# Finishing rows 0 to 3 of a batch during row 7's first pass, and rows 4 to 7 together at the end, in a cached-attention decode kernel

## The chip, the cores and the metric

The kernel runs on one core of a Trainium2 chip. The time is the device time of the program in microseconds (us), as a median of several executions. A profiled execution also has a span, from its first to its last instruction, which is about 2 us shorter than the device time of the same execution. In the lines of the profile PE is TensorE, which does the matmuls, PEld its weight loads, DVE is VectorE, ACT ScalarE, POOL GpSimd, and SP issues the loads.

## The reference

Two identical layers are applied to x, which has 8 batch rows of one token with 448 features. Each layer is an attention over a cache and then a mixer with two small MLPs.

```python
def A(x, k_cache, v_cache, wq, wo):      # caches: 8 rows x 8 kv heads x 4096 x 256, bf16
    q = (x @ wq).reshape(8, 1, 16, 256)  # 16 query heads, 2 per kv head
    p = softmax(q k^T / 16)              # per row and head, over 4096 positions
    return (p v).reshape(8, 1, 4096) @ wo

def B(x, w1, w2, w3, w4):
    ...                                  # hs is zero here: each shift of a 1-token sequence pads it away
    x1 = x + hs
    return x1 + gelu(layernorm(x1) @ w3) @ w4

for _ in range(2):
    x = x + A(layernorm(x), k_cache, v_cache, wq, wo)
    x = x + B(layernorm(x), w1, w2, w3, w4)
return x
```

Both layers read the same caches. The query of the second layer depends on the whole first layer of the same row, so each row's cache is passed over twice. Rows are independent of each other.

## The kernel before

The caches are cut into chunks of 1 MB (128 partitions of 4096 bf16 values). For a pair of kv heads there are 4 key chunks and 4 value chunks. All chunks go through 15 slots in SBUF. A list of items, one per chunk, alternates a key chunk of one pair with a value chunk of the pair before. A slot goes to the next load when its chunk has been used. For each row, 12 of the 32 chunks of the first pass stay in slots (or in PSUM) until the second pass, and so are loaded only once.

```python
kept = [(GP - 1, kv, n) for n in range(4) for kv in range(2)] + [(GP - 2, 0, n) for n in range(3)]
...
for b in range(Bn):                      # (pass, row, pair of kv heads)
    tasks += [(1, b, gp) for gp in keep[::-1]]
    if b + 1 < Bn:
        tasks += [(0, b + 1, gp) for gp in keep]
    if b == Bn - 2:
        tasks += [(1, Bn - 3, free[-1])]
    ...
```

Work that is not tied to a chunk is written as Python generators and is dealt out in pieces between the items. `chain` takes a row from the first pass to the query of the second. `last` ends the attention of a row's second pass. `rest` finishes rows: the product with wo, the normalization, w3, tanh (as gelu), w4. In this kernel it does so for rows 0 to 6 together, begins when row 6 has finished its second pass, and so runs among the chunks of row 7's second pass.

```python
def rest(b, st):
    nb = Bn - 1
    yield from out_cols(lambda i: OT2[:, i % 2, i // 2, :nb], wo_sb, NB2, 0, nb, 1)   # 160 matmuls
    yield from mlp(0, nb)                                                          # 56 with w3, 70 with w4
    ...                                    # 4 matmuls turn the result into rows
    nc.sync.dma_start(out[:nb].rearrange("b s d -> (b s) d"), xo)
...
elif done == 4 and not final:
    add_gen("last", b, last(b, st), idx + 1, idx + (7 if b == Bn - 2 else 13), 6)
    if b == Bn - 2:
        add_gen("last", 0, rest(b, st), idx + 1, len(items) - 2, 21)
```

A row's normalization takes its reciprocal root on POOL, as a power:

```python
nc.vector.tensor_scalar(ve[:, 0], var, 0.0, EPS, ALU.max, ALU.add)
if twice:
    nc.vector.tensor_scalar(ve[:, 1], var, 0.0, EPS * EPS / (1 + EPS), ALU.max, ALU.add)
nc.gpsimd.tensor_tensor(rs[:, 0:n] ..., ve[:, 0:n] ..., nhalf[:].to_broadcast([128, n * nb]), ALU.pow)
```

After the last chunk, row 7 alone goes through what I call the tail: scaling, the last quarter of its wo product, normalization, w3, tanh, w4, and the output.

```python
xs = xT[:, :, Bn - 1 : Bn]
nc.vector.tensor_add(xs, xs, st["y"])
ident2 = ...; nc.vector.tensor_copy(ident2, identb[:])
nc.vector.memset(o_row, 0.0)
HT = run(mlp_hidden(Bn - 1, 1))
...                                        # 14 matmuls with xT, 56 with HT and w4, into o_row
nc.vector.tensor_copy(xo, o_row)
nc.sync.dma_start(out[Bn - 1] ..., xo ...)
```

The softmax here doesn't subtract the row's maximum and nothing guards it: scores larger than these inputs give would overflow.

Of the kernel before, what the change touches and what calls it, by code (L numbers as in the profile page):

```python
# [17 lines left out]
def kernel(  # L18
# [56 lines left out]

    spare = [slots[-1], slots[-2]]

    def scratch(a, n):
        return spare[0][:].bitcast(FP32)[:, a : a + n]

# [26 lines left out]
        ALU.add,  # L107
    )

    ptw = consts.tile([128, 4, 16, 14], BF16, name="ptw")  # L110
    nc.vector.memset(ptw[:], 0.0)

    misc = psum.tile([128, 512], FP32, name="misc")
    ot_bank = misc[:, 256:320]
# [6 lines left out]
    def room_ps(what, nb):  # L121

        at, n = {"y": (320, 8), "st": (336, 2), "h": (352, HC), "q": (384, NB2)}[what]
        if nb == 1:
            return misc[:, at : at + n]
        at, n = {"y": (0, 8), "st": (64, 2), "h": (80, HC), "q": (256, NB2)}[what]
        return store[0 if nb == Bn else 1][:, at : at + n * nb]

    wv = consts.tile([128, 4], FP32, name="wv")
    nc.vector.memset(wv[:, 0:3], 1.0 / D)  # L130
# [1 line left out]
    one = consts.tile([128, 1], FP32, name="one")  # L132
    nc.vector.memset(one[:], 1.0)
    ones = one[:].to_broadcast([128, 128])
    nhalf = consts.tile([128, 1], FP32, name="nhalf")
    nc.vector.memset(nhalf[:], -0.5)
    xb = {}
# [53 lines left out]
    def norm(x, nb, twice):  # L191
# [2 lines left out]

        def room(name, shape, at):
            n = shape[0] * shape[1]
            if nb == 1:
                t = chn.tile([128, n], FP32, tag=name)
                ap = t[:]
            else:  # L200
                ap = scratch(at, n * nb)
            return ap.rearrange("p (s f b) -> p s f b", s=shape[0], f=shape[1])
# [140 lines left out]
    def mlp_hidden(b0, nb):  # L343

        yield from norm(xT[:, :, b0 : b0 + nb], nb, True)
        h_ps = room_ps("h", nb)
        for c in range(HC):
            for fc in range(4):
                w, xi = wblk(w3_sb, F, c, fc)
                nc.tensor.matmul(  # L350
                    h_ps[:, c * nb : c * nb + nb],
                    w,
                    xbs(nb)[:, xi, :],
                    start=(fc == 0),
                    stop=(fc == 3),
                )
            if c == HC // 2:
                yield
        yield
        if nb == 1:  # L360
            g_t = chn.tile([128, 2, HC], FP32, tag="g")
            HT_t = chn.tile([128, HC, 1], BF16, tag="HT")
            hh, g0, HT = g_t[:, 0], g_t[:, 1], HT_t[:]
        else:
            hh, g0 = scratch(64, HC * nb), scratch(640, HC * nb)
            HT = scratch(256, HC * nb // 2).bitcast(BF16).rearrange("p (c b) -> p c b", b=nb)

        nc.vector.tensor_scalar_mul(hh, h_ps, 0.5)
        nc.vector.scalar_tensor_tensor(g0, hh, 2 * 0.044715, h_ps, ALU.mult, ALU.mult)
        nc.vector.scalar_tensor_tensor(g0, g0, 1.0, h_ps, ALU.add, ALU.mult)  # L370
        nc.scalar.activation(g0, g0, ACT.Tanh, scale=0.7978845608028654)
        yield
        nc.vector.scalar_tensor_tensor(
            HT.rearrange("p c b -> p (c b)"), g0, 1.0, hh, ALU.add, ALU.mult
        )
        yield
        return HT

# [84 lines left out]
    def first_last(b, st):  # L463

        yield from half(st["o", 1], st["z"], 1, OT2[:, :, :, b])
        if b == Bn - 1:
            yield from add_cols(
                st["y"],
                lambda i: OT2[:, i % 2, i // 2, b : b + 1],
                wo_sb,  # L470
                range(NB2 // 2, NB2),
                2,
                open=(claim(st), False),
            )
# [5 lines left out]
    def last(b, st):  # L480
        yield from half(st["o", 0], st["z"], 0, OT2[:, :, :, b])

    def rest(b, st):

        nb = Bn - 1
        yield from out_cols(lambda i: OT2[:, i % 2, i // 2, :nb], wo_sb, NB2, 0, nb, 1)
        yield from mlp(0, nb)
        xh = scratch(768, 2 * nb).bitcast(BF16).rearrange("p (c b) -> p c b", c=4)
        nc.vector.tensor_copy(xh, xT[:, :, :nb])
        yield  # L490
        o_row = store[0][:nb, 0:D]
        for fc in range(4):
            w = 128 if fc < 3 else 64
            nc.tensor.matmul(
                o_row[:, 128 * fc : 128 * fc + w], xh[:w, fc, :], identb[:w, :w], start=True, stop=True
            )
        yield
        xo = scratch(1024, D // 2).bitcast(BF16)[:nb]
        nc.vector.tensor_copy(xo, o_row)
        nc.sync.dma_start(out[:nb].rearrange("b s d -> (b s) d"), xo)  # L500



    keep = sorted({gp for gp, _, _ in kept})
    free = [gp for gp in range(GP) if gp not in keep]
    assert Bn > 2 and free == [0, 1] and GP == 4
    tasks = [(0, 0, gp) for gp in free + keep] + [(0, 1, gp) for gp in free]


# [115 lines left out]
    def pv(o_ps, v, a, gp, begin):  # L625


        g = 2 * gp + a // 2
        w = 6 - 2 * (g % 4)
        for y in range(16):  # L630
            q = y % 4
            nc.tensor.matmul(  # L632
                o_ps[32 * q : 32 * q + 8, 0:256],
                ptw[:, a, 4 * (y % 4) + y // 4, w : w + 8],
                v[:, y * Dh : (y + 1) * Dh],
                start=(begin and y < 4),
                stop=(y >= 12),
                skip_group_check=True,
            )
# [40 lines left out]

    def step(idx):

        for kind in ("chain", "last"):
            e = next((e for e in gens if e["kind"] == kind), None)
            if e is None:
                continue
            if e["n"] == 0:
                e["at"] = max(e["at"], idx)
            if e["n"] < e["of"] * (idx - e["at"] + 1) / max(e["until"] - e["at"], 1):
                e["n"] += 1  # L690
                if next(e["g"], gens) is gens:
                    gens.remove(e)

    first_of = {}
    for idx, (n, kv, c) in enumerate(items):
        first_of.setdefault((tasks[n][:2], kv), idx)
    yF, rz_gp, at_end = None, None, False

    for idx, it in enumerate(items):
        n, kv, c = it  # L700
        ps, b, gp = tasks[n]
        p = where[(b, gp), (kv, c)] if ps == 1 and (stays(it) or inside(it)) else where[it]
        slot = slots[p]
        final = (ps, b) == (1, Bn - 1)
        if kv == 0:
# [11 lines left out]
            if "z" not in st:  # L717
                z_t = chn.tile([128, 2, GP], FP32, tag="zall", bufs=3)
                st["z"] = z_t
                if final:  # L720
                    st["y"] = store[2][:, 0:4].unsqueeze(2)
                    oc = store[3][:, 0 : 2 * Hq].rearrange("p (j h) -> p j h", j=2)
            if not (ps == 1 and stays(it)):
                transpose_k(slot)
# [12 lines left out]
        else:  # L737
# [6 lines left out]
            if final and gp in free:  # L744
                pv_cols(oc, slot, c, gp)
                if c % 2 == 1:
# [4 lines left out]
                    run(  # L751
                        add_cols(
                            st["y"],
                            lambda i: OT2[:, i % 2, i // 2, b : b + 1],
                            wo_sb,
                            range(h0, h0 + 4),
                            5,
# [14 lines left out]
            if c == 3:  # L772
# [3 lines left out]
                elif done == 2:  # L776
                    add_gen("chain" if final else "last", b, first_last(b, st), idx + 1, idx + 13, 9)
                elif done == 4 and ps == 0:
                    add_gen("chain", b, chain(b, st), idx + 1, first_of[(1, b), 0] - 1, 30)
                elif done == 4 and not final:  # L780
                    add_gen("last", b, last(b, st), idx + 1, idx + (7 if b == Bn - 2 else 13), 6)
                    if b == Bn - 2:
                        add_gen("last", 0, rest(b, st), idx + 1, len(items) - 2, 21)
        if not (ps == 0 and stays(it)):
            if (ps, gp, kv, c) == (1, keep[-1], 0, 0):
                kept_place = p
            elif final and stays(it) and at_end is not None:

                if not at_end:
                    at_end, spare[:] = True, []  # L790
                spare.append(slot)
                if len(spare) == 2:
                    at_end = None
            else:
                places.append(p)
        emit_loads()
# [2 lines left out]
        step(10 * len(items))  # L799


    xs = xT[:, :, Bn - 1 : Bn]
    nc.vector.tensor_add(xs, xs, st["y"])
    ident2 = spare[1][:, 0:256].bitcast(FP32)
    nc.vector.tensor_copy(ident2, identb[:])
    W = D // 4
    o_row = store[0][:, 0:W]
    nc.vector.memset(o_row, 0.0)
    HT = run(mlp_hidden(Bn - 1, 1))
    for q in range(4):  # L810
        for fc in range(4):
            w = 128 if fc < 3 else 64
            lo, hi = max(W * q, 128 * fc), min(W * q + W, 128 * fc + w)
            if lo < hi:
                nc.tensor.matmul(
                    o_row[32 * q : 32 * q + 1, lo - W * q : hi - W * q],
                    xT[:w, fc, Bn - 1 : Bn],
                    ident2[:w, lo - 128 * fc : hi - 128 * fc],
                    start=(lo == W * q),
                    stop=False,  # L820
# [2 lines left out]
    for c in range(HC):  # L823
        for q in range(4):
            nc.tensor.matmul(
                o_row[32 * q : 32 * q + 1, :],
                HT[:, c, :],
                w4_sb[:, c, W * q : W * q + W],
                start=False,
                stop=(c == HC - 1),  # L830
                skip_group_check=True,
            )
    xo = spare[1][:, 256 : 256 + W]
    nc.vector.tensor_copy(xo, o_row)
    nc.sync.dma_start(
        out[Bn - 1].rearrange("s (q w) -> (s q) w", q=4),
        xo.rearrange("(q r) w -> q r w", r=32)[:, 0, :],
    )


# [28 lines left out]
```

## Time and profile before

| | before |
|---|---|
| device time, median of the 3 runs known for the prediction | 1141.98 us (1140.06 to 1143.87) |
| span of the profiled execution | 1133.7 us |
| last value chunk landed | 1113.3 us |
| its matmuls began, ended | 1121.0, 1122.0 us |
| from there to the end (the tail) | 11.7 us |

The first lines are from the page: the span in 40 slices of 28.3 us, with TensorE's and the DMA engines' busy tenths and the rate of the loads, and the shares of the chain of waits that ended last.

```profile
PE   3145677557764666556764576737665576557786
DMA  9999999999999999999999999999999999999992
GB/s 350 369 421 420 413 369 384 418 417 377 404 419 412 395 398 419 420 408 391 410 419 420 407 393 395 420 419 386 412 418 420 406 379 407 419 417 370 412 419 93
...
DMA 63%; PE 15%; DVE 13%; issue 4%; SPq 3%; ACT 1%; POOL 1%; POOLq 0%; DVEq 0%; ACTq 0%
```

Loading bounds the kernel. The DMA engines are busy in every slice but the last. A chunk lands every 2.5 us at 420 GB/s, and the rate dips to between 369 and 395 GB/s about once per row. TensorE is busy about six tenths. So the time can only change through the landing of the last chunk, or through what comes after it.

These are lines of the timeline of the end: start, duration, engine, line of the kernel, operation, operands, count, and in brackets the idle time of the engine before them. L646 is the value product of the last pairs (32 matmuls a chunk), L332 the product with wo.

```profile
1112.67 0.51 PE L646 MATMUL store<-ptw,slot 128*128 128x2 bf16 x14 [1.79 <-issue]
...
1115.76 1.01 PE L646 MATMUL store<-ptw,slot 128*128 128x2 bf16 x32
...
1118.08 1.01 PE L646 MATMUL store<-ptw,slot 128*128 128x2 bf16 x32
...
1120.10 1.87 PE L646 MATMUL store<-ptw,slot 128*128 128x2 bf16 x64
...
1122.22 0.82 PE L332 MATMUL store<-qT,wo_sb 128*128 128x1 bf16 x20 [0.26 <-DVE qT L410]
...
1125.51 0.70 POOL L236 TENSOR_TENSOR t<-t,nhalf 128x2 f32<-128x2 f32 x1 [35.31 <-DVE t L243]
...
1130.83 0.28 DVE L834 CAST slot<-store 128x112 bf16<-128x112 f32 x1 [1.58 <-PE store L825]
```

The four last value chunks landed at 1105.3, 1107.8, 1110.2 and 1113.3 us. The matmuls of the four last value chunks start at 1115.8, 1118.1, 1120.1 and 1121.0 us, with no bracket that names a load. TensorE is 7.7 us late for the last chunk. From 1122.0 us on, a serial chain runs to the end.

What TensorE waited for in the last row, from 1060 us to the end, with total, number and longest wait (the four largest):

```profile
PE sc L577 <- issue: 4.4, 3, 1.8
PE misc L350 <- DVE xb L253: 1.9, 1, 1.9
PE store L646 <- issue: 1.8, 1, 1.8
PE store L332 <- issue: 1.8, 2, 1.3
```

No load is among them, nor among the smaller ones. "issue" is time without any wait that the profile shows; experiment e9 looks at it.

### The profile page before, as it was taken

How to read it: one execution, taken by the hardware profiler on the slowest of the kernel's cores; microseconds unless marked ns; L12 is line 12 of the kernel's file. 1: busy time of each engine (PE TensorE's matmuls, PEld its weight loads, DVE VectorE, ACT ScalarE, POOL GpSimd, SP SyncE). 2: the span in 40 equal slices, each digit the busy share in tenths (PEclk: the TensorE clock that was granted, in tenths of full speed). 3: DMA queues.
4: the chain of work that ended last, by engine and by line, in shares of the span. 5: the costliest groups of instructions: out<-in, count | busy, mean ns of one | idle time of the engine just before them, and what ended most of it. 6: DMA issues, size and time to landing. Idle time of an engine off the chain costs nothing.

```text
span 1133.7 us, 36989 instructions
## 1 busy us (share of the span) xinstructions
PE 704.3 (62%) x17177; PEld 509.5 (45%) x17177; DVE 593.8 (52%) x1007; ACT 124.3 (11%) x362; POOL 15.6 (1%) x25
## 2 busy tenths in 40 slices
PE   3145677557764666556764576737665576557786
PEld 2123455335543445344542454525444355436566
DVE  5145454545555554646465554645555455555462
ACT  0001001110200011000110011101010101010110
POOL 0000000000000000000000000000000000000000
PEclk9999998655755558555565556555575557555655
DMA  9999999999999999999999999999999999999992
GB/s 350 369 421 420 413 369 384 418 417 377 404 419 412 395 398 419 420 408 391 410 419 420 407 393 395 420 419 386 412 418 420 406 379 407 419 417 370 412 419 93
DMA packets 67199, 449.15 MB, mean 396 GB/s; under 512 B 6871, under 2 KB 12902, under 8 KB 13414
## 3 DMA queue, kind: packets, MB, share of 16 engines
q1 hardware_dynamic: 67046, 446.80, 97.6%
q8 instruction: 134, 2.20, 0.8%
q14 instruction: 19, 0.16, 0.0%
HBM read 446.77 MB, written 0.01 MB: 394 GB/s over the span
## 4 chain that ended last, share of the span: by engine, by line
DMA 63%; PE 15%; DVE 13%; issue 4%; SPq 3%; ACT 1%; POOL 1%; POOLq 0%; DVEq 0%; ACTq 0%
DMA slot<-in_A_k_cache_dram 59%; DVE slot L569 11%; PE sc L577 5%; DMA slot<-in_A_v_cache_dram 4%; PE o L632 3%; SPq L152 2%; PE misc L332 2%; PE store L332 1%; DMA wq_sb<-in_A_wq_dram 1%; SPq L561 1%; PE misc L350 1%; PE store L646 1%; DVE qbd L304 1%; ACT p_n L586 0%; PE misc L278 0%
## 5 line engine op out<-in xcount | busy, mean ns | idle before, releaser
L569 DVE STREAM_TRANSPOSE slot<-slot 128x1024 uint32<-128x1024 uint32 x400 | 472.8, 1222 | 337.1 <-DMA slot<-in_A_k_cache_dram 322.6
L577 PE MATMUL sc<-slot,qbd 128*8 128x128 bf16 x8192 | 277.5, 286 | 322.9 <-DVE slot L569 260.3
L577 PEld LDWEIGHTS <-qbd 128*8 128x8 bf16 x8192 | 188.5, 105 | 409.6 <-issue 214.6
L632 PE MATMUL o<-slot,ptw 128*8 128x256 bf16 x3968 | 242.5, 386 | 54.6 <-DMA slot<-in_A_v_cache_dram 27.2
L586 ACT ACTIVATE p_n<-sc 128x256 bf16<-128x256 f32 x128 | 95.6, 747 | 736.7 <-PE sc L577 736.5
L632 PEld LDWEIGHTS <-ptw 128*8 128x8 bf16 x3968 | 107.9, 109 | 94.2 <-issue 46.1
L332 PEld LDWEIGHTS <-wo_sb 128*128 128x128 bf16 (+1 forms) x1600 | 64.2, 123 | 15.1 <-issue 14.2
L332 PE MATMUL misc<-OT,wo_sb 128*128 128x1 bf16 (+1 forms) x1280 | 55.1, 176 | 2.5 <-issue 2.5
L620 ACT CAST ptw<-misc 128x128 bf16<-128x128 f32 x64 | 17.6, 274 | 233.8 <-PE misc L613 178.4
L278 PEld LDWEIGHTS <-wq_sb 128*128 128x128 bf16 x1152 | 33.4, 104 | 21.3 <-issue 12.5
L403 DVE RECIPROCAL rz<-misc 128x8 f32<-128x8 f32 (+1 forms) x33 | 6.3, 191 | 63.3 <-PE misc L400 63.3
L278 PE MATMUL misc<-xb,wq_sb 128*128 128x1 bf16 x1024 | 31.6, 165 | 5.6 <-DVE xb L253 3.4
L586 ACT ACTIVATION_READ_ACCUMULATOR p_n<-sc 128x1 f32 x128 | 33.7, 264 | 0.0
L431 PEld LDWEIGHTS misc<-R,o_sb 128*128 128x128 f32 x124 | 26.7, 300 | 12.3 <-issue 10.3
L332 PEld LDWEIGHTS <-w_sb 128*128 128x128 bf16 (+1 forms) x630 | 26.7, 125 | 11.9 <-issue 11.3
L431 PE MATMUL misc<-R,o_sb 128*128 128x8 f32 x124 | 29.6, 349 | 1.1 <-ACT o_sb L426 1.1
L332 PE MATMUL misc<-HT_t,w_sb 128*128 128x1 bf16 (+1 forms) x560 | 24.5, 177 | 3.1 <-issue 1.3
L236 POOL TENSOR_TENSOR t<-t,nhalf 128x2 f32<-128x2 f32 (+1 forms) x17 | 10.7, 630 | 1060.1 <-DVE t L243 965.0
L304 DVE TENSOR_SCALAR qbd<-misc,quad 128x64 bf16<-128x64 f32 x64 | 13.8, 277 | 21.1 <-PE misc L298 21.1
L604 DVE STREAM_TRANSPOSE slot<-store 128x512 uint32<-128x512 uint32 x32 | 20.1, 685 | 7.6 <-PE sc L577 7.6
L350 PEld LDWEIGHTS <-w_sb 128*128 128x128 bf16 x560 | 17.5, 104 | 13.4 <-issue 12.9
L400 PE MATMUL misc<-zm,one 128*128 128x8 f32 (+1 forms) x66 | 18.3, 350 | 7.4 <-ACT ptw L620 7.4
(99 smaller groups left out, 254.4 us busy)
## 6 DMA issues: line engine op xcount, KB each, us to landing
slot<-in_A_v_cache_dram SPq DMA_DIRECT2D x216, 1024.0 KB, 10.9
slot<-in_A_k_cache_dram SPq DMA_DIRECT2D x200, 1024.0 KB, 14.1
wo_sb<-in_A_wo_dram SPq DMA_DIRECT2D x1, 3584.0 KB, 26.8
wq_sb<-in_A_wq_dram SPq DMA_DIRECT2D x3, 1024.0 KB, 6.9
w_sb<-in_B_w_dram SPq DMA_DIRECT2D x1, 1568.0 KB, 13.0
w_sb<-in_B_w_dram SPq DMA_DIRECT2D x3, 448.0 KB, 26.8
wq_sb<-in_A_wq_dram SPq DMA_DIRECT2D x2, 256.0 KB, 10.2
w_sb<-in_B_w_dram SPq DMA_DIRECT2D x2, 112.0 KB, 9.3
```

Of the source, the lines that this page charges most:

```text
L152: nc.sync.dma_start(t[:, fc * cols : (fc + 1) * cols], src[fc * 128 : fc * 128 + 128, :])
L278: nc.tensor.matmul(q_ps[:, j * Hq + h, :], w, xbs(nb)[:, xi, :], start=(fc == 0), stop=(fc == 3),)
L304: nc.vector.tensor_scalar_mul(qbd[:, :, :, a, :], qs.rearrange("p e (f g u h) -> p (e f) u g h", f=2, u=2, h=2)[:, :, u], quad[:, a : a + 1],)
L332: nc.tensor.matmul(r, w[:, i, lo:hi], rhs(i), start=start, stop=stop, skip_group_check=open is not None,)
L350: nc.tensor.matmul(h_ps[:, c * nb : c * nb + nb], w, xbs(nb)[:, xi, :], start=(fc == 0), stop=(fc == 3),)
L400: nc.tensor.matmul(z_ps, ones, zm[:], start=True, stop=True)
L431: nc.tensor.matmul(ot_ps[:, j], o_sb[:, 128 * j : 128 * j + 128], R[:], start=True, stop=True)
L569: nc.vector.transpose(w, w)
L577: nc.tensor.matmul(sc[32 * k : 32 * k + 8, 128 * x : 128 * x + 128], qbd[:, ep, gp].rearrange("p a h -> p (a h)"), kv[:, k, 2 * half + e2, ...
L586: nc.scalar.activation(p_sb[:, :, :, 2 * u : 2 * u + 2].rearrange("p t i x -> p x t i"), sc[:, 256 * u : 256 * u + 256].rearrange("p (x t ...
L604: nc.vector.transpose(slot[:].bitcast(U32)[:, 512 * n : 512 * n + 512], store[n][:].bitcast(U32))
L632: nc.tensor.matmul(o_ps[32 * q : 32 * q + 8, 0:256], ptw[:, a, 4 * (y % 4) + y // 4, w : w + 8], v[:, y * Dh : (y + 1) * Dh], start=(begin ...
```

## The change

The intent is to finish rows 0 to 3 earlier, where TensorE has time, and to let rows 4 to 7 share the tail. The rest of the diff makes that possible: PSUM and SBUF room for four rows, a narrower tile for the probabilities to pay for it, and a zeroed tile HTw in which the finished rows stay zero, so that one final product with w4 serves all eight rows.

```diff
+    MID = Bn // 2
...
-    ptw = consts.tile([128, 4, 16, 14], BF16, name="ptw")
+    ptz = consts.tile([128, 520], BF16, name="ptw")       # windows of 8 columns now overlap
...
+    HTw = consts.tile([128, HC, Bn], BF16, name="HTw")
+    nc.vector.memset(HTw[:], 0.0)
...
-    def rest(b, st):
-        nb = Bn - 1
-        yield from out_cols(lambda i: OT2[:, i % 2, i // 2, :nb], wo_sb, NB2, 0, nb, 1)
-        yield from mlp(0, nb)
-        ...                                               # to rows, and their own output DMA
+    def rest():
+        yield from out_cols(lambda i: OT2[:, i % 2, i // 2, :MID], wo_sb, NB2, 0, MID, 1)
+        yield from mlp(0, MID)
+        nc.vector.memset(HTw[:, :, 0:MID], 0.0)
+        yield
...
+        if (ps, b, gp, kv, c) == (0, Bn - 1, REST, 0, 0):
+            assert pairs_done[1, MID - 1] == 4
+            add_gen("rest", 0, rest(), idx + 1, idx + 18, 21)
...
-                            lambda i: OT2[:, i % 2, i // 2, b : b + 1],
+                            lambda i: OT2[:, i % 2, i // 2, MID:],
...
-                    if b == Bn - 2:
-                        add_gen("last", 0, rest(b, st), idx + 1, len(items) - 2, 21)
...
-            elif final and stays(it) and at_end is not None:
-                ...                                       # two slots of the last row held back as scratch
...
-    xs = xT[:, :, Bn - 1 : Bn]
+    xs = xT[:, :, MID:]
...
-    HT = run(mlp_hidden(Bn - 1, 1))
+    run(mlp_hidden(MID, Bn - MID))
...
-    nc.sync.dma_start(out[Bn - 1] ..., xo ...)
+    for q in range(4):
+        (nc.scalar if q % 2 else nc.sync).dma_start(
+            out[:, 0, W * q : W * q + W], xo[32 * q : 32 * q + Bn]
+        )
```

Matmul counts in the tail stay the same: its matmuls have four columns, or weights of eight columns, where they had one.

More of the change, by code (lines that the diff above doesn't have):

```diff
@@ L108 @@
     )
-    ptw = consts.tile([128, 4, 16, 14], BF16, name="ptw")
-    nc.vector.memset(ptw[:], 0.0)
+    ptz = consts.tile([128, 520], BF16, name="ptw")
+    nc.vector.memset(ptz[:], 0.0)
+    ptw = ptz[:, 0:512].rearrange("p (a n w) -> p a n w", a=4, w=8)
     misc = psum.tile([128, 512], FP32, name="misc")
@@ L125, in room_ps @@
             return misc[:, at : at + n]
+        if nb < Bn:
+            at = {"y": 416, "st": 456, "h": 128}[what]
+            return misc[:, at : at + n * nb]
         at, n = {"y": (0, 8), "st": (64, 2), "h": (80, HC), "q": (256, NB2)}[what]
-        return store[0 if nb == Bn else 1][:, at : at + n * nb]
+        return store[0][:, at : at + n * nb]
     wv = consts.tile([128, 4], FP32, name="wv")
@@ L196, in room @@
             n = shape[0] * shape[1]
-            if nb == 1:
-                t = chn.tile([128, n], FP32, tag=name)
-                ap = t[:]
+            if nb < Bn:
+                t = chn.tile([128, n * MID], FP32, tag=name)
+                ap = t[:, 0 : n * nb]
             else:
@@ L359, in mlp_hidden @@
         yield
+        g_t = chn.tile([128, 2, HC * MID], FP32, tag="g")
+        hh, g0 = g_t[:, 0, 0 : HC * nb], g_t[:, 1, 0 : HC * nb]
         if nb == 1:
-            g_t = chn.tile([128, 2, HC], FP32, tag="g")
             HT_t = chn.tile([128, HC, 1], BF16, tag="HT")
-            hh, g0, HT = g_t[:, 0], g_t[:, 1], HT_t[:]
+            HT = HT_t[:]
         else:
-            hh, g0 = scratch(64, HC * nb), scratch(640, HC * nb)
-            HT = scratch(256, HC * nb // 2).bitcast(BF16).rearrange("p (c b) -> p c b", b=nb)
+            HT = HTw[:, :, b0 : b0 + nb]
         nc.vector.tensor_scalar_mul(hh, h_ps, 0.5)
@@ L373, in mlp_hidden @@
         nc.vector.scalar_tensor_tensor(
-            HT.rearrange("p c b -> p (c b)"), g0, 1.0, hh, ALU.add, ALU.mult
+            HT,
+            g0.rearrange("p (c b) -> p c b", b=nb),
+            1.0,
+            hh.rearrange("p (c b) -> p c b", b=nb),
+            ALU.add,
+            ALU.mult,
         )
@@ L481, in last @@
         yield from half(st["o", 0], st["z"], 0, OT2[:, :, :, b])
-    def rest(b, st):
-        nb = Bn - 1
-        yield from out_cols(lambda i: OT2[:, i % 2, i // 2, :nb], wo_sb, NB2, 0, nb, 1)
-        yield from mlp(0, nb)
-        xh = scratch(768, 2 * nb).bitcast(BF16).rearrange("p (c b) -> p c b", c=4)
-        nc.vector.tensor_copy(xh, xT[:, :, :nb])
-        yield
-        o_row = store[0][:nb, 0:D]
-        for fc in range(4):
-            w = 128 if fc < 3 else 64
-            nc.tensor.matmul(
-                o_row[:, 128 * fc : 128 * fc + w], xh[:w, fc, :], identb[:w, :w], start=True, stop=True
-            )
-        yield
-        xo = scratch(1024, D // 2).bitcast(BF16)[:nb]
-        nc.vector.tensor_copy(xo, o_row)
-        nc.sync.dma_start(out[:nb].rearrange("b s d -> (b s) d"), xo)
+    def rest():
+        yield from out_cols(lambda i: OT2[:, i % 2, i // 2, :MID], wo_sb, NB2, 0, MID, 1)
+        yield from mlp(0, MID)
+        nc.vector.memset(HTw[:, :, 0:MID], 0.0)
+        yield
     keep = sorted({gp for gp, _, _ in kept})
@@ L506 @@
     assert Bn > 2 and free == [0, 1] and GP == 4
+    REST = keep[0]
     tasks = [(0, 0, gp) for gp in free + keep] + [(0, 1, gp) for gp in free]
@@ L628, in pv @@
         g = 2 * gp + a // 2
-        w = 6 - 2 * (g % 4)
         for y in range(16):
             q = y % 4
+            at = 128 * a + 8 * (4 * q + y // 4) + 6 - 2 * (g % 4)
             nc.tensor.matmul(
                 o_ps[32 * q : 32 * q + 8, 0:256],
-                ptw[:, a, 4 * (y % 4) + y // 4, w : w + 8],
+                ptz[:, at : at + 8],
                 v[:, y * Dh : (y + 1) * Dh],
@@ L681, in step @@
     def step(idx):
-        for kind in ("chain", "last"):
+        for kind in ("chain", "last", "rest"):
             e = next((e for e in gens if e["kind"] == kind), None)
@@ L696 @@
         first_of.setdefault((tasks[n][:2], kv), idx)
-    yF, rz_gp, at_end = None, None, False
+    rz_gp = None
     for idx, it in enumerate(items):
@@ L720 @@
                 if final:
-                    st["y"] = store[2][:, 0:4].unsqueeze(2)
+                    st["y"] = store[2][:, 0 : 4 * (Bn - MID)].rearrange("p (f b) -> p f b", f=4)
                     oc = store[3][:, 0 : 2 * Hq].rearrange("p (j h) -> p j h", j=2)
@@ L753 @@
                             st["y"],
-                            lambda i: OT2[:, i % 2, i // 2, b : b + 1],
+                            lambda i: OT2[:, i % 2, i // 2, MID:],
                             wo_sb,
@@ L786 @@
                 kept_place = p
-            elif final and stays(it) and at_end is not None:
-                if not at_end:
-                    at_end, spare[:] = True, []
-                spare.append(slot)
-                if len(spare) == 2:
-                    at_end = None
             else:
@@ L799 @@
         step(10 * len(items))
-    xs = xT[:, :, Bn - 1 : Bn]
+    end = [slots[p] for p in places[:2]]
+    xs = xT[:, :, MID:]
     nc.vector.tensor_add(xs, xs, st["y"])
-    ident2 = spare[1][:, 0:256].bitcast(FP32)
+    ident2 = end[0][:, 0:256].bitcast(FP32)
     nc.vector.tensor_copy(ident2, identb[:])
@@ L815 @@
                 nc.tensor.matmul(
-                    o_row[32 * q : 32 * q + 1, lo - W * q : hi - W * q],
-                    xT[:w, fc, Bn - 1 : Bn],
+                    o_row[32 * q : 32 * q + Bn, lo - W * q : hi - W * q],
+                    xT[:w, fc, :],
                     ident2[:w, lo - 128 * fc : hi - 128 * fc],
@@ L825 @@
             nc.tensor.matmul(
-                o_row[32 * q : 32 * q + 1, :],
-                HT[:, c, :],
+                o_row[32 * q : 32 * q + Bn, :],
+                HTw[:, c, :],
                 w4_sb[:, c, W * q : W * q + W],
@@ L832 @@
             )
-    xo = spare[1][:, 256 : 256 + W]
+    xo = end[1][:, 0:W]
     nc.vector.tensor_copy(xo, o_row)
-    nc.sync.dma_start(
-        out[Bn - 1].rearrange("s (q w) -> (s q) w", q=4),
-        xo.rearrange("(q r) w -> q r w", r=32)[:, 0, :],
-    )
+    for q in range(4):
+        (nc.scalar if q % 2 else nc.sync).dma_start(
+            out[:, 0, W * q : W * q + W], xo[32 * q : 32 * q + Bn]
+        )
 _INS = ['A_x', 'A_k_cache', 'A_v_cache', 'A_wq', 'A_wo', 'B_x', 'B_w1', 'B_w2', 'B_w3', 'B_w4']
```

## The prediction

> **What bounds the kernel now.** Loading. The page's slices show the DMA engines at 9 tenths in all slices but the last, about 420 GB/s where nothing holds it; the chain of waits is 63% DMA, almost all key chunks. A 1 MB chunk lands every 2.5 us. The packets show the last value chunk landing at about 1111.6 us of the 1133.7 us span. So only two things can move the time: when that load lands, and what follows it.
>
> **The end before.** After 1111.6 us there are 22 us without loads. TensorE is late: in the timeline the matmuls of the last four value chunks start at 1115.8, 1118.1, 1120.1 and 1121.0 us, about 9 to 12 us after each chunk landed (1104.1, 1106.6, 1109.1, 1111.6). This lag arises from 1064 us on, where the finish of rows 0 to 6 (160 matmuls with wo, 56 with w3, 70 with w4, 4 to transpose) is mixed into the last row's work. In the windows from 1060 to 1110 us TensorE is busy 73 to 90%, and these 290 matmuls take about 12 us of it (64 wo matmuls 2.9 us, w4 70 in 3.3 us with gaps, w3 56 in 1.7 us), with instruction gaps ("issue") of 1 to 2 us. From the end of the last value matmul (1122.0 us) to the end is a serial tail of 11.7 us: scale, wo, norm, w3, tanh, w4, output.
>
> **What the change does.**
> 1. It takes those 290 matmuls out of the last row's second pass; without them TensorE needs about 3 us per key/value pair against 4.9 us of loading, so it should catch up well before 1110 us and start the last value chunk on landing, about 1111.8, ending about 1112.8 instead of 1122.0: -9.2 us, all on the critical path.
> 2. It lengthens the serial tail, now for 4 rows: the POOL power goes from 2 to 8 elements (0.70 and 1.64 us in the trace): +0.9 us; wider DVE steps, two instead of one for the variance: about +0.4 us. Matmul counts stay (4 columns cost as 1; 56 w3 matmuls took 1.66 us with one column, 54 of them about 1.6 us with seven). Four output DMAs on two queues instead of one: a second issue on a queue costs up to the 0.61 us seen: +0.4 us. (The Trainium skill, "Trainium Kernel Development and Optimization", Key Constraints: issuing from several engines only saves issue time.) Together +1.7 us.
> 3. It puts 286 matmuls for rows 0 to 3 (about 12 us) at about 958 to 990 us, the first pass of row 7, third and fourth pair of heads. There TensorE is busy 19.6 of 30 us, so it fills up and lags some us; loads there have free slots and run at 420 GB/s, and 990 to 1010 us has TensorE only 43% busy, so nearly all is absorbed. Cost 0 to 3 us, I take +1.
> 4. Narrower probability tile, new memsets: nothing.
>
> Sum: -9.2 + 1.7 + 1 = -6.5 us of 1133.7, 0.6%. From 1141.98: 1135.5 us, range 1130.5 to 1141.5. Chances: faster by over 2% 0.01, within 2% 0.97, slower 0.02.
>
> **What would show it.** Right: last chunk still lands near 1112 us; its matmuls start within 2 us of landing; the tail from there is about 13.4 us; POOL in it 1.6 us; GB/s at 960 to 1000 us stays near 420; the span is near 1127 us.
>
> **What would make it wrong.** The lag at 960 to 1000 us holds slots back, so that loading slips by more than 3 us and the last landing moves; TensorE doesn't catch up in the last pass because instruction gaps, not the removed matmuls, hold it; the four small output DMAs cost more than estimated.

## More of the kernel before

The moment at which a load has landed is not a line of the profile. I take it from the packets: each load ends with four-byte completion writes, one from each DMA engine that took part, and the 16th of a load is its landing. ("The Trainium skill", page "DMA: Bandwidth & Descriptors", section "Why a DMA increments its semaphore by 16 and not by 1", says that only the full 16 means that all data has landed, and that a transfer may use fewer engines. The trace agrees: there are 6867 such writes on the load queue for 428 loads of 16, the 8-row load of x with 8, and the outputs with 7 and 4.)

## The result, and the profile after

The six runs of the changed kernel have a median of 1131.66 us (1129.84 to 1134.41), and six runs of the kernel before have 1141.02 us. The ratio is 0.9923, with a 95% interval of 0.9898 to 0.9947. A ratio compares the runs of the two kernels in the same rounds, so it is not quite the ratio of the medians. Two later sets of rounds, on two chips, gave 0.9940 and 0.9957. The change gains about 0.4 to 0.8%: each interval lies below 1.

The loads of the changed kernel, and TensorE's busy tenths, from its page:

```profile
PE   3145677557755677556774667647666477758866
DMA  9999999999999999999999999999999999999994
GB/s 352 371 420 419 413 370 397 419 414 386 402 419 420 388 414 419 419 404 408 410 420 420 386 388 415 419 420 386 385 408 419 413 360 409 418 419 373 405 420 178
```

The pattern of the loads is unchanged. TensorE's busy tenths rise from 5 to 7 in the 35th slice (959 to 987 us) and fall from 8 to 6 in the 39th (1072 to 1100 us): that is the moved work. The same end in the timeline (L647 is the value product, L340 the product with wo, L244 the power):

```profile
1108.03 1.01 PE L647 MATMUL store<-ptw,slot 128*128 128x2 bf16 x32
...
1110.35 1.01 PE L647 MATMUL store<-ptw,slot 128*128 128x2 bf16 x32
...
1112.38 1.01 PE L647 MATMUL store<-ptw,slot 128*128 128x2 bf16 x32
...
1113.87 1.01 PE L647 MATMUL store<-ptw,slot 128*128 128x2 bf16 x32 [0.47 <-DMA slot<-in_A_v_cache_dram]
...
1115.14 0.82 PE L340 MATMUL store<-qT,wo_sb 128*128 128x4 bf16 x20 [0.26 <-DVE qT L423]
...
1118.68 1.65 POOL L244 TENSOR_TENSOR t<-t,nhalf 128x8 f32<-128x8 f32 x1 [75.18 <-DVE t L251]
...
1125.08 0.27 DVE L830 CAST slot<-store 128x112 bf16<-128x112 f32 x1 [1.59 <-PE store L821]
```

The last chunk landed at 1113.4 us, as before. TensorE now waits for it (the bracket names the load) and begins 0.5 us after the landing. The power takes 1.65 us instead of 0.70. TensorE's waits from 1060 us on:

```profile
PE sc L578 <- DVE slot L570: 10.8, 10, 2.8
PE misc L358 <- DVE xb L263: 2.9, 1, 2.9
PE o L633 <- DMA slot<-in_A_v_cache_dram: 2.1, 2, 1.4
...
PE store L647 <- DMA slot<-in_A_v_cache_dram: 0.5, 1, 0.5
```

Now the loads, and VectorE's transposition of each key chunk as it arrives (L570), are what TensorE waits for in the last row. The span fell by 5.6 us, from 1133.7 to 1128.1. The sum is simple: the last value matmuls end 7.1 us earlier (1122.0 to 1114.9), and the tail is 1.5 us longer (11.7 to 13.2).

In the new place of `rest`, here are windows of 10 us before the change: length, busy time of each engine with its number of instructions, granted clock, DMA share, GB/s.

```profile
960.00:970.00 10.00, 8.21 (x217) 6.32 (x218) 5.93 (x6) 1.11 (x3) 0.00 (x0) 0.63 1.02 422
970.00:980.00 10.00, 6.28 (x129) 3.94 (x127) 6.46 (x10) 1.42 (x5) 0.00 (x0) 0.50 1.01 418
980.00:990.00 10.00, 5.12 (x108) 3.44 (x100) 6.22 (x8) 0.88 (x4) 0.00 (x0) 0.50 1.01 422
```

And the same windows after it:

```profile
960.00:970.00 10.00, 6.66 (x180) 5.65 (x177) 3.85 (x4) 0.74 (x2) 0.00 (x0) 0.57 1.01 419
970.00:980.00 10.00, 8.88 (x182) 6.97 (x178) 4.47 (x13) 0.74 (x2) 0.71 (x1) 0.50 1.01 419
980.00:990.00 10.00, 8.67 (x207) 6.65 (x206) 7.62 (x21) 1.43 (x5) 0.93 (x1) 0.56 1.02 421
```

TensorE (first column) goes from 5 to 6 tenths to nearly 9 in the second and third window. In the packets and the timeline together, it starts a chunk up to 11.9 us after its landing there, where it had been 1 to 3 us, and is back at 3.1 us at about 1004 us. The loads go on at about 420 GB/s.

### The profile page after: what moved, and what is told of

The parts are those of the page before. It is cut to its first block, busy times and chain, and to the rows that moved or that the text cites. A ratio compares the mean times of both kernels' runs of the same rounds, so it can differ in the third digit from the quotient of the medians. Undisturbed runs are those within 1.5% of the kernel's fastest.

```text
span 1128.1 us, 36985 instructions
## 1 busy us (share of the span) xinstructions
PE 705.9 (63%) x17173; PEld 510.5 (45%) x17173; DVE 591.8 (52%) x1009; ACT 123.9 (11%) x362; POOL 15.7 (1%) x25
## 5 line engine op out<-in xcount | busy, mean ns | idle before, releaser
L570 DVE STREAM_TRANSPOSE slot<-slot 128x1024 uint32<-128x1024 uint32 x400 | 472.3, 1221 | 329.9 <-DMA slot<-in_A_k_cache_dram 318.1
L340 PEld LDWEIGHTS <-wo_sb 128*128 128x128 bf16 (+1 forms) x1600 | 64.0, 123 | 17.1 <-issue 16.0
L340 PE MATMUL misc<-OT,wo_sb 128*128 128x1 bf16 (+1 forms) x1280 | 54.9, 176 | 4.2 <-issue 4.2
L340 PEld LDWEIGHTS <-w_sb 128*128 128x128 bf16 (+1 forms) x630 | 26.1, 124 | 9.8 <-issue 9.3
L244 POOL TENSOR_TENSOR t<-t,nhalf 128x2 f32<-128x2 f32 (+2 forms) x18 | 13.3, 739 | 1098.8 <-DVE t L251 1002.0
L340 PE MATMUL misc<-HT_t,w_sb 128*128 128x1 bf16 (+1 forms) x560 | 24.4, 177 | 2.5 <-ACT ptw L621 1.2
## 6 DMA issues: line engine op xcount, KB each, us to landing
slot<-in_A_v_cache_dram SPq DMA_DIRECT2D x216, 1024.0 KB, 11.9
```

What stands on the lines that cost most here:

```text
L340: nc.tensor.matmul(r, w[:, i, lo:hi], rhs(i), start=start, stop=stop, skip_group_check=open is not None,)
L570: nc.vector.transpose(w, w)
```

## The experiments

Loading itself varies between executions: in the traces below the last chunk lands anywhere from 1113.3 to 1122.5 us with no change that would touch the loads, most of it gathered before 960 us. The timed ratios therefore have intervals of about 0.3 to 0.6% to each side. I read each trace relative to its own landings. The columns are the landing of the last chunk, the start of its matmuls, how late that is, the end of the matmuls, the tail (span less that end, from rounded times), and the span. The last column is a stretch of loading: from the landing of row 7's first key chunk of pair 2, first pass, at about 955 us, to the last landing. It shows whether loads were held up in between.

| kernel | landed | start | late by | end | tail | span | loading stretch |
|---|---|---|---|---|---|---|---|
| before | 1113.3 | 1121.0 | 7.7 | 1122.0 | 11.7 | 1133.7 | 159.9 |
| after | 1113.4 | 1113.9 | 0.5 | 1114.9 | 13.2 | 1128.1 | 160.1 |
| after_again | 1120.7 | 1121.1 | 0.5 | 1122.2 | 13.1 | 1135.3 | 161.8 |
| e1_rest_late | 1113.7 | 1120.5 | 6.8 | 1121.5 | 13.1 | 1134.6 | 161.3 |
| e2_no_rest | 1116.3 | 1116.8 | 0.5 | 1117.9 | 13.1 | 1131.0 | 160.1 |
| e3_before_no_rest | 1116.7 | 1117.2 | 0.5 | 1118.2 | 11.7 | 1129.9 | 160.6 |
| e4_hold_slots | 1122.5 | 1123.0 | 0.5 | 1124.0 | 13.2 | 1137.2 | 162.1 |
| e5_rest_tight | 1126.9 | 1127.4 | 0.5 | 1128.4 | 13.2 | 1141.6 | 167.6 |
| e6_rest_row6 | 1118.8 | 1119.2 | 0.5 | 1120.3 | 13.2 | 1133.5 | 160.7 |
| e9_shift | 1122.2 | 1128.8 | 6.7 | 1129.8 | 11.7 | 1141.5 | 161.1 |
| after_third | 1115.5 | 1116.0 | 0.5 | 1117.0 | 13.2 | 1130.2 | 161.1 |
| e8_split_hoist | 1116.1 | 1116.5 | 0.5 | 1117.5 | 12.4 | 1129.9 | 161.3 |

The first four experiments ran on one chip, the next four on another, the last two on a third, each set beside the kernel before.

### after_again: the changed kernel as a yardstick

No edit.

> The changed kernel once more, as the yardstick of this chip. Theory A (the gain is TensorE arriving on time at the end, because the finish of the earlier rows no longer runs in the last row): ratio to the kernel before 0.990 to 0.995, first matmul of the last value chunk within 1.5 us of its landing, about 13.2 us from the end of the last value matmul to the end of the span. Every rival expects the same of this run.

Measured: ratio 0.9940 (0.9887 to 0.9992), late by 0.5 us, tail 13.1 us. As expected. Its span, 1135.3 us, is longer than that of the first profile of the kernel before (1133.7 us), although it is the faster kernel: its last chunk landed 7.4 us later. A single span does not decide here; the ratio of the same rounds and the lateness do.

### e1_rest_late: the same work back in the last row

```diff
-        if (ps, b, gp, kv, c) == (0, Bn - 1, REST, 0, 0):
-            assert pairs_done[1, MID - 1] == 4
-            add_gen("rest", 0, rest(), idx + 1, idx + 18, 21)
...
                     add_gen("last", b, last(b, st), idx + 1, idx + (7 if b == Bn - 2 else 13), 6)
+                    if b == Bn - 2:
+                        add_gen("rest", 0, rest(), idx + 1, len(items) - 2, 21)
```

> The changed kernel, but the finish of rows 0 to 3 (286 matmuls) put back into the last row's second pass; everything else of the change stays (four rows at the end, one output step, two slots no longer held back). Theory A: TensorE is late again, the first matmul of the last value chunk 5 to 9 us after its landing, and the tail stays 13.2 us, so the span is 1133 to 1138 us and the ratio to the kernel before 0.998 to 1.006. Rival B (the gain comes from the output step or from the two slots given back to the loads): as fast as the changed kernel, ratio 0.990 to 0.995. Rival C (7 rows at once were the trouble, 4 are light): lag under 3 us, ratio below 0.997.

Measured: ratio 1.0006 (0.9962 to 1.0050), late by 6.8 us, tail 13.1 us. Theory A is met. Rival B, the output step or the slots, falls, since both are still as the change has them. Rival C falls too: four rows make TensorE about as late as seven, which fits that the number of matmuls is nearly the same (286 against 290). TensorE's timeline in the last row:

```profile
1093.47 0.38 PE L633 MATMUL o<-slot,ptw 128*8 128x256 bf16 x2 [2.96 <-issue]
...
1112.28 0.41 PE L647 MATMUL store<-ptw,slot 128*128 128x2 bf16 x10 [1.85 <-issue]
...
1119.60 1.87 PE L647 MATMUL store<-ptw,slot 128*128 128x2 bf16 x64
```

The last two value chunks are again taken in one row of 64 matmuls, without a wait for a load. The gaps named "issue" are back too.

### e2_no_rest: what the work costs in its new place

```diff
-        if (ps, b, gp, kv, c) == (0, Bn - 1, REST, 0, 0):
-            assert pairs_done[1, MID - 1] == 4
-            add_gen("rest", 0, rest(), idx + 1, idx + 18, 21)
```

The result of rows 0 to 3 is wrong.

> The changed kernel without any finish of rows 0 to 3 (their result is wrong on purpose). It measures what these 286 matmuls cost in their new place. Theory A: nothing that lasts; the last value chunk lands within 1.5 us of where it does in the changed kernel, and the ratio to the kernel before lies within 0.003 of the changed kernel's of the same rounds. Rival D (the new place costs, and a better place would gain more): faster than the changed kernel by 3 us or more, with all loads after 960 us landing earlier.

Measured: ratio 0.9964 (0.9907 to 1.0021) against 0.9940 of the changed kernel in the same rounds, so within the 0.003 expected. Late by 0.5 us, tail 13.1 us, loading stretch 160.1 us. The last chunk did not land within 1.5 us of where it had in either trace of the changed kernel (1116.3 us, against 1113.4 and 1120.7), so that part of the expectation was too narrow for the scatter of loading; the stretch is the better measure. It is 161.3 us on average in the five traces that do the work there (after, after_again, e4, after_third, e8), and 160.6 us in the six that do not (before, e1, e2, e3, e6, e9). The difference of about 0.7 us lies inside a scatter of 1 to 2 us, so no cost of the new place is shown. Rival D falls: dropping the work altogether gains nothing that could be measured.

### e3_before_no_rest: the removal alone, in the old kernel

```diff
-                    if b == Bn - 2:
-                        add_gen("last", 0, rest(b, st), idx + 1, len(items) - 2, 21)
```

This is the edit to the kernel before. Rows 0 to 6 are neither finished nor written (wrong); the tail for one row, the held slots and the old probability tile stay.

> The kernel before without the finish of rows 0 to 6 and without their output (wrong on purpose); one row in the tail as before, two slots held back as before, old probability tile. Theory A: removing these 290 matmuls alone gives the whole gain: the last value chunk's matmuls start within 1.5 us of its landing, the tail stays 11.7 us, span about 1126.6 us (1125 to 1129), ratio 0.987 to 0.994, so at or slightly below the changed kernel. Rival B (slots or output step): no more than a third of the gain, ratio above 0.997.

Measured: ratio 0.9941 (0.9890 to 0.9991), span 1129.9 us, late by 0.5 us, tail 11.7 us. Lateness and tail are as expected. The span is 0.9 us over its range and the ratio a hair over, because this execution's last chunk landed at 1116.7 us, 3.4 us later than in the profile from which I had worked out 1126.6. Taking the finish of rows 0 to 6 from the last row removes the lateness by itself, without any other part of the change. The edit takes out the steps of the finish on the other engines too, as e1 puts them back; but TensorE waited only 0.2 us for those in the last row (L350 for xb in the kernel before), so they are not what made it late.

### e4_hold_slots: two slots held back again

```diff
             if (ps, gp, kv, c) == (1, keep[-1], 0, 0):
                 kept_place = p
+            elif final and stays(it) and at_end is not None:
+                ...                              # as in the kernel before
...
-    end = [slots[p] for p in places[:2]]
+    end = spare
```

> The changed kernel, but two slots of the last row's kept chunks are held back from the loads again, as the kernel before does. Theory A: no effect, all the last 20 loads are queued in time anyway: from the landing of the last row's first loaded key chunk (pair 2, quarter 3) to the last landing 47 to 50 us as in every run so far (48.7 before, 47.6 changed), lag of the last chunk under 1.5 us, tail 13.1 us. Rival B (giving the two slots back is part of the gain): that stretch at least 2 us longer than the changed kernel's, or ratio near 1.

Measured: ratio 0.9933 (0.9872 to 0.9993). The stretch of the last 20 loads took 48.3 us (48.7 before, 47.6 in the first profile of the changed kernel, 48.3 in after_again), late by 0.5 us, tail 13.2 us. The slots have no effect that shows. Rival B falls in its second half too.

### e5_rest_tight: the same work where slots are scarce

```diff
-        if (ps, b, gp, kv, c) == (0, Bn - 1, REST, 0, 0):
+        if (ps, b, gp, kv, c) == (1, Bn - 3, free[-1], 0, 0):
             assert pairs_done[1, MID - 1] == 4
-            add_gen("rest", 0, rest(), idx + 1, idx + 18, 21)
+            add_gen("rest", 0, rest(), idx + 1, idx + 8, 21)
```

> The changed kernel with the finish of rows 0 to 3 begun some 30 us later, at the first key chunk of row 5's delayed pair, and pressed into 8 items (about 20 us), where only 4 of 15 slots rotate because the kept chunks fill the others. Theory A says that the place was free because loads there had many free slots; so here TensorE's lag must hold up loads: GB/s falls below 400 at 990 to 1020 us, and the stretch from the landing of row 7's first kept-stage key chunk (first pass, pair 2) to row 6's first key chunk of the second pass plus the stretch to the last landing (160 to 162 us in all four changed or reduced runs) grows by 3 to 9 us; last lag still under 1.5 us, tail 13.1 us. Rival E (any place outside the last row is as good): stretch stays 160 to 162 us.

Measured: ratio 1.0010 (0.9954 to 1.0067). Windows of this run:

```profile
1005.00:1015.00 10.00, 7.76 (x158) 5.97 (x147) 3.70 (x12) 0.74 (x2) 0.99 (x1) 0.50 1.02 423
1015.00:1025.00 10.00, 6.17 (x168) 4.60 (x167) 6.38 (x15) 1.27 (x5) 0.65 (x1) 0.50 0.83 328
1025.00:1035.00 10.00, 7.62 (x155) 6.50 (x156) 5.17 (x9) 1.01 (x3) 0.00 (x0) 0.50 0.69 230
1035.00:1045.00 10.00, 7.73 (x183) 5.86 (x181) 4.53 (x16) 0.62 (x2) 0.69 (x1) 0.50 0.95 350
```

And of the changed kernel, where the same loads land about 6 us earlier:

```profile
1010.00:1020.00 10.00, 5.97 (x106) 4.00 (x106) 5.40 (x10) 1.29 (x4) 0.00 (x0) 0.50 0.97 391
1020.00:1030.00 10.00, 8.33 (x194) 6.66 (x194) 5.72 (x19) 0.74 (x2) 0.70 (x1) 0.50 0.99 370
1030.00:1040.00 10.00, 7.91 (x194) 5.83 (x193) 5.04 (x15) 1.23 (x4) 0.00 (x0) 0.50 0.99 374
```

The loads fall to 230 GB/s for 10 us, and the loading stretch grows to 167.6 us, about 6 us more than in the others. The dip begins only at about 1015 us, at the end of the stretch that I had named for it (990 to 1020 us). The times at which the loads were issued and landed show why. From 960 to 992 us each load was issued about 19 us before it landed, so several were queued. After that a load was issued only every 4 to 8 us, where 2.5 us keeps pace, and those issued at 1024 to 1029 us landed 4.5 us later: the queue was used up. In the changed kernel this lead shrank from 19 us to 10 us while the work ran, and the loads went on at 417 to 421 GB/s. At the end everything is as in the changed kernel (late by 0.5 us, tail 13.2 us), yet the whole gain is gone. Rival E falls. The place matters, and it matters through the slots. One thing moved with it: the work was also packed into fewer items, so how much belongs to the density and how much to the scarcity of slots was not separated.

### e6_rest_row6: the same stage, one row earlier

```diff
-        if (ps, b, gp, kv, c) == (0, Bn - 1, REST, 0, 0):
+        if (ps, b, gp, kv, c) == (0, Bn - 2, REST, 0, 0):
```

> The changed kernel with the finish of rows 0 to 3 one row earlier, in the same stage of row 6's first pass (third pair of heads on). Theory A: the same slack exists in every row, so the same as the changed kernel: last lag under 1.5 us, tail 13.1 us, ratio to before 0.988 to 0.998, and the stretch from row 7's first kept-stage key chunk to the last landing 160 to 162 us. Rival F (row 7 is special, because its chain of the first pass is shorter or longer there): landing of that chunk relative to the same chunk of row 6 is over 3 us longer than in the kernel before.

Measured: ratio 0.9938 (0.9891 to 0.9986), late by 0.5 us, tail 13.2 us, stretch 160.7 us; from row 6's chunk to row 7's 115.4 us, and 115.5 us in the kernel before. Rival F falls: the same stage of row 6 absorbs the work as well.

### e9_shift: what the gaps without a wait are

```diff
+    for _ in range(64):
+        nc.tensor.matmul(misc[:, 128:136], identb[:], identb[:, 0:8], start=True, stop=True)
     ps0 = rows_to_cols(x_row, Bn)
```

This is the edit to the kernel before.

> The kernel before with 64 more matmuls (128 TensorE instructions with their weight loads) in the prologue. TensorE's gaps without any wait sit at the 193rd of every 256 TensorE instructions in all six traces so far (20 to 28 gaps above 0.9 us in each). If they belong to a boundary of the instruction stream, they stay at the 193rd of 256 by count and so move by 128 instructions in the program: other lines and other matmuls of the last row pause. If they belong to the work at those places (a hidden wait for a tile), they stay with that work, and move to the 65th of 256 by count. Lag of the last chunk 5 to 10 us and tail 11.7 us in either case.

Measured: one run of unknown state, 1143.37 us; late by 6.7 us, tail 11.7 us. In the trace of the kernel before, 27 gaps of TensorE above 0.9 us end exactly at instruction 193 of a block of 256 (counted from 0, weight loads and semaphore instructions included); no other place in the block has more than 3. In this run 18 do, again at 193. One gap is in both traces. In the kernel before it is the first line of the timeline shown above, after 18 of the 32 matmuls of a value chunk, and it ends with TensorE's instruction number 33729. In this run:

```profile
1115.76 0.72 PE L332 MATMUL store<-qT,wo_sb 128*128 128x1 bf16 x22
1118.28 0.41 PE L332 MATMUL store<-qT,wo_sb 128*128 128x1 bf16 x10 [1.80 <-issue]
```

The gap of 1.80 us ends with instruction 33729 again, but that is now in the wo product, 128 instructions earlier in the program. So the gaps belong to the count, a boundary in the instruction stream, and not to the work there. "The Trainium skill", page "Runtime: NRT & Kernel Launch", section "Instruction fetch mechanics", says that instructions are fetched in blocks of 16 KiB, that is 256 instructions, and that this is mostly hidden. The trace agrees with the block (the instruction queue has 134 packets, 2.20 MB in all) and not always with the hiding.

The packets of the instruction queue, set beside the timeline, settle what these gaps are. Their number follows TensorE's instructions, one for each full 256: 134 for 34500 in the kernel before, 132 for 33916 in e2 and e3, 135 for 34628 in e9. In the kernel before, 26 of the 27 gaps end 1.2 to 1.6 us after such a packet has landed (the 27th is the wait at the very end of the program). In none of the twelve traces does a block of 256 begin less than 1.2 us after its packet. So TensorE was waiting for its instructions.

They also show more than the gaps do. In the kernel before, nine blocks in a row, up to the one that begins at 1112.7 us, took 6.0 to 6.6 us each from one beginning to the next, and every one began 1.2 to 1.6 us after its packet had landed, with or without a gap above 0.9 us. In the last row TensorE thus ran at the pace at which its instructions came, about 256 in 6.2 us. In e1 and e9 it is much the same. In the changed kernel only four of the eight blocks of that stretch begin within 1.7 us of their packet; before the one at 1091.1 us the packet had been there for 6.8 us, and TensorE was waiting for loads. So gaps and matmuls are not rivals: at that pace the 572 instructions of 286 matmuls are about 14 us (an estimate, 572 / 256 blocks of 6.2 us). Why the next packet starts only 3.5 to 4.2 us after a block has begun is not shown.

Gaps alone do not make TensorE late. From 1060 us to 1113 us the kernel before has six such gaps above 0.9 us, 8.6 us together; from 1060 us to its last landing the changed kernel has none in its first profile, three (4.4 us) in after_again and two (2.7 us) in after_third, and was late by 0.5 us each time. In e2 and e3 there are three (5.7 and 5.5 us), and TensorE was late by 0.5 us there too, while e9 with three (5.6 us) was late by 6.7 us. So TensorE catches up with some gaps present once the finish is gone.

### e8_split_hoist and after_third: a shorter tail

What the change made worse is the tail, and its largest added term is the power of 8 elements on POOL. Only 4 of the 8 are needed for the next matmuls.

```diff
-        nc.vector.tensor_scalar(ve[:, 0], var, 0.0, EPS, ALU.max, ALU.add)
         if twice:
             nc.vector.tensor_scalar(ve[:, 1], var, 0.0, EPS * EPS / (1 + EPS), ALU.max, ALU.add)
+        nc.vector.tensor_scalar(ve[:, 0], var, 0.0, EPS, ALU.max, ALU.add)
...
-        nc.gpsimd.tensor_tensor(rs[:, 0:n] ..., ve[:, 0:n] ..., ..., ALU.pow)
+        for k in (1, 0) if twice else (0,):
+            nc.gpsimd.tensor_tensor(rs[:, k], ve[:, k], nhalf[:].to_broadcast([128, nb]), ALU.pow)
...
+    ident2 = ...; nc.vector.tensor_copy(ident2, identb[:])     # moved up, with the memset of o_row
     xs = xT[:, :, MID:]
     nc.vector.tensor_add(xs, xs, st["y"])
```

> A version meant to beat both: the changed kernel, whose tail is now the part that grew. The POOL power is split in two, the four elements that the next matmuls wait for first, the other four behind it; and the identity copy and the clearing of the output bank are issued on VectorE before the tail's first addition instead of after it. Theory A (the tail is a serial chain behind the last landing): POOL on the chain 1.0 us instead of 1.65, 0.2 us less on VectorE, tail 12.3 us (12.0 to 12.6) instead of 13.1 to 13.2; last lag still 0.5 us. 0.8 us is 0.07% and too small for the timed ratio, which is expected at 0.989 to 0.996; the tail is read from the trace. If the tail stays above 12.8 us, the power was not what the chain waited for.

> The changed kernel again beside it, to compare tails and ratios of the same chip: tail 13.1 to 13.2 us, last lag 0.5 us, ratio 0.989 to 0.996.

Measured, five rounds on one chip: ratio to the kernel before 0.9937 (0.9911 to 0.9963) for the version, 0.9957 (0.9932 to 0.9982) for the changed kernel; medians 1131.52 and 1132.29 us. The tail is 12.4 us against 13.2 us. Lines of its timeline (x2: both powers, of which the matmuls wait for the first):

```profile
1116.52 1.01 PE L645 MATMUL store<-ptw,slot 128*128 128x2 bf16 x32 [1.18 <-DMA slot<-in_A_v_cache_dram]
...
1121.09 2.00 POOL L245 TENSOR_TENSOR t<-t,nhalf 128x4 f32<-128x4 f32 x2 [75.50 <-DVE t L249]
1122.15 0.43 DVE L261 SCALAR_TENSOR_TENSOR xb<-t 128x12 bf16<-128x12 f32 x3 [1.06 <-POOL t L245]
```

VectorE goes on 1.06 us after the powers began, instead of 1.68 us. The version is correct, its tail is shorter by the 0.8 us expected, and it is faster than the kernel before. Against the changed kernel the gain is read from the trace only; the intervals of the two ratios overlap.

## Why the prediction was right

The prediction was 1135.5 us, a change of -0.6%, with 1130.5 to 1141.5 as range; the measured median is 1131.66 us and the ratio 0.9923. In the profiled pair the span changed by -5.6 us where the prediction's sum was -6.5 us. Part of this closeness is luck: the gain was set about 2 us too high, and the two costs together about 1.1 us too high. Point by point:

1. *"What bounds the kernel now. Loading."* Right. The lines of the loads are alike before and after, and whatever moved the last landing (e5, or plain scatter between executions) moved the span.
2. *"-9.2 us, all on the critical path."* The mechanism was right, and e1 and e3 show it from both sides: with the matmuls in the last row TensorE is 6.8 to 7.7 us late, without them 0.5 us. The size was too large: it measured 7.1 us (1122.0 to 1114.9). The step that failed is *"the last value chunk landing at about 1111.6 us"*. I had counted completion writes in sixteens from the first load on, but the first load has 8 rows and only 8 writes, so each landing was read from the middle of its load. The chunk landed at 1113.3 us. The prediction named "instruction gaps, not the removed matmuls" as what would make it wrong. The packets in e9 show that the two belong together: in the last row TensorE ran at the pace of its instructions, and the matmuls were 572 of them.
3. *"POOL power goes from 2 to 8 elements (0.70 and 1.64 us in the trace): +0.9 us"*: 1.65 us were measured. For the whole tail +1.7 us were predicted and 1.5 us came. The four output DMAs were over-estimated: from the end of the last copy to the end of the span it is 2.6 us before (1131.1 to 1133.7) and 2.7 us after (1125.4 to 1128.1), where +0.4 us had been set. The section "Key Constraints" on the page "Trainium Kernel Development and Optimization" of the Trainium skill, which says that issuing from several engines only saves issue time, is in line with this: the pairs of issues took 0.66 us on the one queue and 0.97 us on the other, side by side. No run issues all four on one queue, so the saving itself was not measured.
4. *"Cost 0 to 3 us, I take +1"* for the new place: about 0.7 us, from the loading stretches of eleven traces, which is not distinguishable from zero. The reason given, free slots, is supported by e5, where the same work among scarce slots costs about 6 us of loading.
5. *"Narrower probability tile, new memsets: nothing."* No run isolates them. e3, which has the old tile, and e2, which has the new one, leave no room for more than the scatter: both are late by 0.5 us, with stretches of 160.6 and 160.1 us.

The timed gain (0.4 to 0.8%, that is 4.9 to 8.8 us, in three sets of rounds) scatters around the -5.6 us of the profiled pair because loading varies by several us between executions. What causes that scatter is open; the traces show it growing before row 7 (the chunk that starts the stretch lands at 952 to 961 us).

## What to carry to other kernels

When loading bounds a kernel, compare each chunk's landing with the start of the work that uses it: a compute engine that is late only at the very end costs all of that lateness, though it is never the bottleneck by busy time. Move work that need not wait for the end to a stage where buffers are plentiful, not merely to where the engine looks idle, because lateness where buffers are scarce comes back as slower loading. Count the instructions that you move, and not only the busy time: in a dense stretch here TensorE went no faster than its instructions came. Then look at what the move leaves in the serial tail, and let the tail's slow steps compute first what the next step waits for.

## What the Trainium skill lacked or had wrong

- "Runtime: NRT & Kernel Launch", section "Instruction fetch mechanics", says that fetch is hidden because instructions are dispatched more slowly than they arrive. Here TensorE paused for more than 0.9 us at 26 boundaries of 256 instructions in the kernel before, each time until 1.2 to 1.6 us after the block's packet had landed; the longest such pause in any trace was 2.98 us (in e3). In the last row nine blocks in a row came at this pace, 6.0 to 6.6 us each.
- "DMA: Bandwidth & Descriptors" gives the number of engines of a transfer correctly, and the trace agrees (8 completion writes for 8 rows). It does not say what this means for reading landings from a trace: counting completions in sixteens without it put the last landing 1.7 us too early in the prediction (1111.6 for 1113.3 us).
- No page found gives the cost of a power on POOL by size. Here it is 0.55, 0.70, 1.02, 1.64 and 2.59 us for 1, 2, 4, 8 and 14 elements per partition, or about 0.16 us per element above a fixed 0.4 us.
